# Dummy matmuls in the head, and full inverse matrices for the last four output pairs of a gated long convolution and MLP

## The chip, the cores and the metric

The kernel runs on one core of one Trainium2 chip. The metric is the device time of one execution in microseconds (us). Five engines of that core matter here: PE (TensorE, the matmuls), DVE (VectorE), ACT (ScalarE), POOL (GpSimd) and SP (SyncE, which starts most transfers). PEld is the weight load of PE, which overlaps the matmuls. "Span" is the time from the first to the last instruction of a profiled execution; the time is some 1.8 us longer than the span. "Granted clock" is the TensorE clock that the profile reports, 1.0 being full speed.

## The reference

Two branches on the same input x, of 2048 rows and 640 columns, are mixed by a gate for each row:

```python
def _A_ref(q, k, v, shift_k, ssm_k, ssm_D):      # long convolution
    ...                                          # k_shift: 4-tap causal filter along the rows of k
    kv = k_shift * v
    ...                                          # y: convolution with ssm_k along the 2048 rows, by FFT of 4096
    y = y + kv * ssm_D[None, None, :]
    return q * y

def _B_ref(x, w1, w2, w3, w4):                   # two MLPs, each with a residual
    h = _gelu(_layernorm(x, axis=-1) @ w1)
    ...                                          # hs: four column groups of h shifted by 1, -1, 2, -2 rows, times w2
    x1 = x + hs
    h2 = _gelu(_layernorm(x1, axis=-1) @ w3) @ w4
    return x1 + h2

g = _sigmoid((x * gate_w).sum(-1, keepdims=True))
return g * a + (1 - g) * b                       # a from _A_ref, b from _B_ref, x is A_q
```

## The kernel before

The kernel records some 1,300 operations, each with the engine it runs on, and a list scheduler written in the same file puts the operations of every engine in order. A table of several hundred numbers, called biases, shifts the priority of groups of operations, and a second table, SHIFTS, that of single ones. The order of each engine is then fixed.

The rows are worked on in 16 tiles of 128 rows. In the head, tile after tile is normalised (DVE), transposed (PE) and copied (ACT), and the first layer starts on narrow blocks of columns:

```python
def ln1(t0, t1):
    for t in range(t0, t1):
        ln_bn(t, X[:, t, :])                     # DVE: statistics, two halves of 320
    bn_math(t0, t1)
    for t in range(t0, t1):
        ...
        ts(xn, x, bna[:, t, 0:1], st[0, 5][:, t:t + 1], ALU.subtract, ALU.mult)   # DVE: normalise
        ...                                      # PE: 5 transposes; ACT: one copy out of PSUM
```

In the tail, the convolution comes back from the frequency domain. `G` holds half an inverse transform: four products give a part `pr[:, 0]` that is even about the middle, four more an odd part `pr[:, 1]`. The sum of the parts is one tile of 128 rows, their difference, turned upside down, is the tile that mirrors it. So 8 matmuls give a pair of tiles of 320 columns, with an add, a subtraction and a matmul with a flip matrix. There are 16 such pairs, `k` = 0 to 15:

```python
def final(hh, c, q, k):
    ts_, td = 4 * c + q, 4 * c + 3 - q           # the two tiles of the pair
    ...
    P.dma(sp, qt, rows(A_q))
    act(qt[:, 0], qt[:, 0], ACTF.Copy, scale=gst[3][:, ts_:ts_ + 1])              # ACT: q * g
    pr = ps(2, "inv")[:, :, 0:320]
    for e in range(2):
        mm(pr[:, e], [(G[:, j, e ^ (j // 2), 128 * q:128 * (q + 1)], XF[:, hh, c, j, e ^ (j // 2), :])
                      for j in range(4)])                                         # PE: 4 matmuls
    pf = ps(1, "fl")[:, 0:320]
    for d in (slice(0, 320),) if k < 15 else (slice(0, 160), slice(160, 320)):
        act(ab[:, :, d], pr[:, :, d], ACTF.Copy)                                  # ACT: both parts
        tt(gy[:, 0, d], ab[:, 0, d], ab[:, 1, d], ALU.add)                        # DVE
        tt(ab[:, 0, d], ab[:, 0, d], ab[:, 1, d], ALU.subtract)                   # DVE
        mm(pf[:, d], [(flip, ab[:, 0, d])])                                       # PE
        act(gy[:, 1, d], pf[:, d], ACTF.Copy, scale=gst[3][:, td:td + 1])         # ACT
        for e in (slice(0, 2),) if k < 14 else (slice(0, 1), slice(1, 2)):
            tt(gy[:, e, d], gy[:, e, d], qt[:, e, d], ALU.mult)                   # DVE
            tt(gy[:, e, d], gy[:, e, d], two(X)[:, e, d], ALU.add)                # DVE
            ...                                                                   # out
```

The helpers `tt`, `act` and `mm` record every operation of their kind, so in the profile all matmuls of `mm` have one line, L1230 before and L1234 after; `tt` is L1210 and L1214, `act` L1220 and L1224. `ts` is L1215 and L1219.

## Time and profile before

| | before |
|---|---|
| time, median of 3 runs | 238.98 us (238.97 to 239.32) |
| span of the profiled execution | 237.2 us |
| PE busy, DVE busy, ACT busy | 221.5, 222.1, 177.8 us |
| inverse products and the first flip after them are through on PE | 226.65 us |
| last DVE operation ends | 234.88 us |

The profile's first lines and its stretches are in the prediction below. Three more readings are needed. The first is the shares of the chain of work that ended last:

```profile
PE 44%; DVE 34%; ACT 14%; issue 4%; DMA 2%; SPq 1%; DVEq 0%
```

The chain passes from engine to engine; none has more than half of it. The second is PE's timeline from 199.80 us on (start, length, line and operation, count, and in brackets the idle time before it and the engine that ended it):

```profile
199.80 26.85 PE L1230 MATMUL PSall<-arena 128*128 128x512 bf16 x189
227.02 0.85 PE L1230 MATMUL PSall<-arena 128*128 128x320 bf16 x5 [0.37 <-DVE arena L1210]
232.02 0.58 PE L1230 MATMUL PSall<-arena 128*128 128x320 bf16 x2 [4.15 <-DVE arena L1210]
233.38 0.31 PE L1230 MATMUL PSall<-arena 128*128 128x160 bf16 x1 [0.77 <-ACT arena L1220]
```

PE has no gap until 226.65 us. What comes after are single flip matmuls that wait for a difference from DVE: in this tail DVE works and PE looks on. After the last product there are 9 flips: pairs 8 to 15, one each, and pair 15, which is cut in two, one more. The first of them has just ended at 226.65 us (the stretch from there on still counts it: 9 matmuls, but 8 weight loads); the lines show the other 8. DVE's last stretch, from the same view, ends at 226.49 + 8.39 = 234.88 us:

```profile
226.49 8.39 DVE L1210 TENSOR_TENSOR arena<-arena 128x160 bf16<-128x160 bf16 x31 [0.19 <-ACT arena L1220]
```

The chain in the prediction passes from DVE to "DVEq" at 234.72 us. That is no end of DVE's work: the view books the last operation itself under that name. The third reading is the timeline of PE in the head, from 13 to 21 us:

```profile
14.49 0.73 PE L1445 MATMUL PSall<-arena 128*128 128x128 bf16 x10 [0.30 <-ACT arena L1220]
15.82 4.53 PE L1230 MATMUL PSall<-arena 128*128 128x320 bf16 x37 [0.60 <-DVE arena L1469]
```

L1445 are the transposes. The 37 matmuls from 15.82 us on are the first group of the second layer, and 4.53 us for them is the rate at full clock.

### The profile page before, as it was taken

Reading aid. Unit: us, or ns where it says so; the run is one execution under the profiler, and the core shown is the slowest. Engines: PE = TensorE matmul, PEld = TensorE weight load, DVE = VectorE, ACT = ScalarE, POOL = GpSimd, SP = SyncE. Lnnn points to the kernel's source line nnn. Section 1 sums busy time; section 2 is a strip of 40 time slices with the busy share of each in tenths; the row PEclk is TensorE's granted clock in tenths of the full one; section 3 lists DMA queues with packets and bytes.
Section 4 is the critical chain, followed back from the end, with each engine's and each line's share of the span. In section 5 each row is a group of like instructions: output and inputs, shape, how many; then the busy total and the mean of one; then the engine's idle time right before and its main releaser. Section 6 shows DMA issues by size and latency. Waiting matters only on the chain.

```text
span 237.2 us, 4158 instructions
## 1 busy us (share of the span) xinstructions
PE 221.5 (93%) x1477; PEld 133.4 (56%) x1488; DVE 222.1 (94%) x418; ACT 177.8 (75%) x328; POOL 92.3 (39%) x116
## 2 busy tenths in 40 slices
PE   5789999999999999999999999999999999999931
PEld 2476875556454555544766546764567744677710
DVE  5899999979998999899999799999999799999996
ACT  2288979986889977999999992557897466326972
POOL 0334928932892246230548304643015414152000
PEclk9999999999999999999999999999999999999995
DMA  6999798999989989986264982799989996899825
GB/s 174 348 373 336 147 253 159 116 222 266 212 196 211 260 195 351 298 214 156 67 99 76 187 178 39 130 174 158 267 150 231 158 192 135 172 157 153 219 81 169
DMA packets 64201, 45.54 MB, mean 192 GB/s; under 512 B 28722, under 2 KB 58932, under 8 KB 64180
## 3 DMA queue, kind: packets, MB, share of 16 engines
q1 hardware_dynamic: 57884, 33.36, 56.1%
q0 software_dynamic: 6112, 11.80, 29.8%
q8 instruction: 12, 0.20, 0.3%
q10 hardware_dynamic: 184, 0.11, 0.2%
q14 instruction: 9, 0.07, 0.1%
HBM read 24.29 MB, written 2.62 MB: 113 GB/s over the span
## 4 chain that ended last, share of the span: by engine, by line
PE 44%; DVE 34%; ACT 14%; issue 4%; DMA 2%; SPq 1%; DVEq 0%
PE PSall L1230 43%; DVE arena L1210 27%; ACT arena L1220 14%; DMA arena<-in_A_q_dram 2%; DVE arena L1400 2%; DVE arena L1469 2%; DVE arena L1215 2%; DVE arena L1504 1%; SPq L239 1%; DVE arena L1401 0%; ACT PSall L1220 0%; PE PSall L1445 0%; DVEq L1687 0%; DVEq L453 0%; DVE arena L1354 0%
## 5 line engine op out<-in xcount | busy, mean ns | idle before, releaser
L1230 PE MATMUL PSall<-arena 128*128 128x320 bf16 (+4 forms) x1411 | 212.5, 309 | 8.6 <-DVE arena L1210 5.1
L1210 DVE TENSOR_TENSOR arena<-arena 128x2560 bf16<-128x2560 bf16 (+6 forms) x263 | 185.1, 762 | 6.5 <-ACT arena L1220 4.7
L1230 PEld LDWEIGHTS PSall<-arena 128*128 128x128 bf16 x1422 | 128.5, 98 | 91.5 <-ACT arena L1220 9.1
L1220 ACT ACTIVATE arena<-PSall 128x640 bf16<-128x640 f32 (+5 forms) x187 | 110.9, 651 | 29.3 <-PE PSall L1230 21.3
L1220 ACT ACTIVATE arena<-arena 128x640 bf16<-128x640 bf16 (+3 forms) x74 | 52.0, 733 | 5.5 <-DVE arena L1210 2.9
L239 POOL DMA_DIRECT2D arena<-arena x30 | 31.2, 1102 | 61.1 <-DVE arena L1210 41.9
L1404 POOL TENSOR_TENSOR arena<-arena 128x1 f32<-128x1 f32 (+1 forms) x26 | 24.9, 964 | 35.7 <-DVE arena L1215 35.4
L1215 POOL TENSOR_SCALAR arena<-arena 128x1 f32<-128x1 f32 (+2 forms) x41 | 26.9, 657 | 26.2 <-ACT arena L1220 8.9
L1220 ACT ACTIVATE arena<-PSall,arena 128x640 bf16<-128x640 f32 (+2 forms) x33 | 20.4, 655 | 19.3 <-PE PSall L1230 19.3
L1400 DVE BATCH_NORM_STATS2 arena<-arena 128x6 f32<-128x320 bf16 x32 | 13.8, 477 | 2.7 <-DMA arena<-in_A_q_dram 2.6
L1215 DVE TENSOR_SCALAR arena<-arena 128x1 f32<-128x1 f32 (+2 forms) x45 | 12.4, 299 | 0.6 <-POOL arena L1215 0.2
L1210 POOL TENSOR_TENSOR arena<-arena 128x1 f32<-128x1 f32 (+1 forms) x15 | 10.0, 670 | 3.3 <-DVE arena L1215 2.6
L1256 PE MATMUL PSall<-arena 128*128 128x512 bf16 x24 | 6.7, 448 | 2.4 <-DVE arena L1252 2.4
L1469 DVE TENSOR_SCALAR arena<-arena 32x256 bf16<-32x256 bf16 (+2 forms) x28 | 6.3, 229 | 1.6 <-ACT arena L1220 1.1
L1504 DVE SCALAR_TENSOR_TENSOR arena<-PSall,arena 128x640 bf16<-128x640 f32 x8 | 6.4, 814 | 0.0
L1256 PEld LDWEIGHTS PSall<-arena 128*128 128x128 bf16 x24 | 2.6, 112 | 6.1 <-DVE arena L1252 2.4
L1220 ACT ACTIVATE PSall<-PSall 128x640 f32<-128x640 f32 x8 | 5.7, 711 | 0.0
L1445 PE MATMUL PSall<-arena 128*128 128x128 bf16 x40 | 3.2, 220 | 1.1 <-DVE arena L1215 0.8
L1445 PEld LDWEIGHTS PSall<-arena 128*128 128x128 bf16 x40 | 2.4, 97 | 2.3 <-DVE arena L1215 1.8
L1259 ACT ACT_TABLE_LOAD x1 | 1.3, 1283 | 2.1 <-issue 2.1
L1401 DVE BATCH_NORM_AGGREGATE arena<-arena 128x2 f32<-128x12 f32 x16 | 2.8, 201 | 0.0
L1220 ACT ACTIVATION_READ_ACCUMULATOR arena<-arena 128x1 f32 x8 | 2.1, 257 | 0.0
(23 smaller groups left out, 8.0 us busy)
## 6 DMA issues: line engine op xcount, KB each, us to landing
arena<-arena POOLq DMA_DIRECT2D x14, 640.0 KB, 6.0
arena<-in_A_k_dram SPq DMA_DIRECT2D x14, 400.0 KB, 4.6
arena<-in_A_q_dram SPq DMA_DIRECT2D x20, 160.0 KB, 5.7
arena<-in_A_ssm_k_dram SPq DMA_DIRECT2D x5, 512.0 KB, 4.8
arena<-in_A_v_dram SPq DMA_DIRECT2D x16, 160.0 KB, 2.9
arena<-arena POOLq DMA_DIRECT2D x16, 160.0 KB, 4.2
out_dram<-arena SPq DMA_DIRECT2D x14, 160.0 KB, 2.0
arena<-in_A_q_dram SPq DMA_DIRECT2D x6, 320.0 KB, 6.2
```

Of the source, the lines that this page charges most:

```text
L239: fn = lambda e: e.dma_start(out, in_, **kw)
L1210: P.op(eng, lambda e: e.tensor_tensor(o, real(a), real(b), op), [a, b], [o], dve_ns(o, [a, b], 2) if eng == "dve" else 500)
L1215: P.op(eng, lambda e: e.tensor_scalar(o, real(a), s1, s2, op0=op0, **({} if op1 is None else {"op1": op1})), [a] + aps, [o], dve_ns(o, [a] ...
L1220: P.op("act", lambda e: e.activation(real(o), real(a), f, bias=bias, scale=scale, **({"accum_out": accum} if accum is not None else {})), ...
L1230: fns.append(lambda e, l=l, r=r, i=i: e.matmul(real(o), l, r, start=(i == 0), stop=(i == last)))
L1256: warmed = P.op("pe", [lambda e: e.matmul(real(pw), warm[:, 0:128], warm[:, 128:640], start=True, stop=True)] * 2, [warm], [pw], 856.0 if ...
L1400: P.op("dve", lambda e, o=o, i=i: e.bn_stats(o, i), [i], [o], 400)
L1401: P.op("dve", lambda e: e.bn_aggr(bna[:, t, :], bns[k]), [bns[k]], [bna[:, t, :]], 120)
L1404: P.op("pool", lambda g: g.tensor_tensor(o, a, e, ALU.pow), [a, e], [o], dur)
L1445: P.op("pe", [lambda e, c=c, pb=pb, xn=xn: e.transpose(real(pb)[:, 128 * c:128 * (c + 1)], xn[:, 128 * c:128 * (c + 1)], ident) for c in r ...
L1469: P.op("dve", lambda e, o=hT[q, 4, c0:c0 + n], i=hx[q, :]: e.tensor_scalar(o, i, 1.0, None, op0=ALU.mult), [hx[q, :]], [hT[q, 4, c0:c0 + n ...
L1504: P.op("dve", lambda e: e.scalar_tensor_tensor(x, real(pr), 1.0, x, op0=ALU.mult, op1=ALU.add, accum_out=st[1, 0][:, t:t + 1]), [pr, x], [ ...
```

## The change

It has two intents: to keep PE busy, and its clock up, between the first tiles' first and second layers; and to relieve DVE and ACT in the tail at PE's expense. Besides, the normalisation of tiles 0 to 2 has its priority raised, and both tables of biases have new values throughout, so that the order of every engine is new. The diff, with the number tables left out:

```diff
+        self.boost = 0.0
-        op.bias += self.biases.get(op.grp, 0.0) + self.opb.get(idx, 0.0)
+        op.bias += self.boost + self.biases.get(op.grp, 0.0) + self.opb.get(idx, 0.0)
     ...
+    def keep_warm(n):
+        done = max(o.idx for o in P.ops if o.eng == "pe" and o.grp.startswith("mm1"))
+        pw = ps(1, "warm")
+        for i in range(n):
+            P.op("pe", [lambda e: e.matmul(real(pw), w1[:, 0, 0:128], w1[:, 0, 128:640], start=True, stop=True)] * 2,
+                 [w1], [pw], 432.0).preds.setdefault(done, False)
     ...
+    DIRECT = 12
+    GT = V(oXT, 2048).rearrange("p (e j q m) -> p e j q m", e=2, j=4, q=2)
+    def turn_inverse():
+        for e in range(2):
+            for j in (0, 2):
+                act(GT[:, e, j:j + 2], G[:, j:j + 2, e ^ (j // 2)].rearrange("p j (q m) -> p j q m", q=2)[:, :, :, ::-1],
+                    ACTF.Copy, scale=1.0 - 2.0 * e)
     def final(hh, c, q, k):
     ...
-        act(qt[:, 0], qt[:, 0], ACTF.Copy, scale=gst[3][:, ts_:ts_ + 1])
+        if k < DIRECT:
+            act(qt[:, 0], qt[:, 0], ACTF.Copy, scale=gst[3][:, ts_:ts_ + 1])
     ...
+        if k >= DIRECT:
+            mm(pr[:, 0], halves[0] + halves[1])                                   # 8 matmuls
+            mm(pr[:, 1], [(GT[:, e, j, q], halves[e][j][1]) for e in range(2) for j in range(4)])
+            for e, t in enumerate((ts_, td)):
+                act(gy[:, e], pr[:, e], ACTF.Copy, scale=gst[3][:, t:t + 1])
+        else:
     ...                                          # as before, without the cutting of pair 15
     for sc in range(4):
     ...
+            P.boost = {0: 4e6, 1: 3e6, 2: 1e6}.get(t[0], 0.0)
             at(ln1, *t)
+            P.boost = 0.0
     ...
+                if (sc, k, i) == (0, 0, 1):
+                    at(keep_warm, 4)
```

`keep_warm(4)` makes 8 matmuls of 512 columns whose result nobody reads. `GT` is `G` with its columns reversed, and with the sign of the odd part turned, so that 8 matmuls with it give the mirrored tile at once, without subtraction or flip. `halves` holds the operands of the four even and the four odd products.

## The prediction

> **What bounds the kernel now.** I read the page's busy shares first, then the chain of work that ended last, then busy time by stretches, and last the timeline and the groups of the final 20 us. The first line of the page says that no single engine is the limit:
>
> ```profile
> PE 221.5 (93%) x1477; PEld 133.4 (56%) x1488; DVE 222.1 (94%) x418; ACT 177.8 (75%) x328; POOL 92.3 (39%) x116
> ```
>
> Two engines are near full at once. Stretches show where the remaining idle time lies (columns: PE, PEld, DVE, ACT, POOL busy, clock, DMA share, GB/s):
>
> ```profile
> 0.00:10.00 10.00, 6.75 (x25) 2.62 (x26) 6.15 (x30) 1.49 (x2) 2.12 (x8) 1.00 0.80 254
> 10.00:15.00 5.00, 4.18 (x69) 3.84 (x70) 4.97 (x19) 4.04 (x13) 1.95 (x5) 1.00 1.08 332
> 15.00:20.00 5.00, 4.40 (x41) 3.52 (x38) 4.93 (x18) 4.10 (x9) 1.33 (x5) 1.00 1.05 378
> ...
> 180.00:210.00 30.00, 29.89 (x189) 18.47 (x189) 28.65 (x36) 16.29 (x29) 9.56 (x10) 1.00 0.90 167
> 210.00:220.00 10.00, 10.00 (x76) 7.11 (x75) 9.60 (x12) 5.21 (x10) 4.73 (x5) 1.00 0.95 165
> 220.00:226.65 6.65, 6.65 (x49) 4.57 (x47) 6.17 (x20) 6.65 (x15) 0.00 (x0) 1.00 0.75 199
> 226.65:235.00 8.35, 1.75 (x9) 0.64 (x8) 8.23 (x31) 4.44 (x11) 0.00 (x0) 0.73 0.40 119
> ```
>
> From 10 us to 226.65 us, taken as one stretch, PE is busy 213.00 of 216.65 us and DVE 207.71. So the middle has 3.65 us of PE gaps and 8.9 us of DVE gaps to give, no more. What is left is the head (PE does only warm-up matmuls before 9.98 us) and the tail: after 226.65 us PE is nearly empty while DVE is full. The chain names the tail's owner, in order of time (start, length, engine and line):
>
> ```profile
> 213.74 2.97 DVE arena L1210 x3
> 216.71 0.02 issue
> 216.73 9.73 ACT arena L1220 x20
> 226.47 0.02 issue
> 226.49 8.24 DVE arena L1210 x30
> 234.72 0.15 DVEq L1687
> ```
>
> The last chained product ends near 218.2 us; from 218.50 to 234.72 DVE does nothing but the output pairs, and ACT is full from 220 us to 226.65. The groups of instructions between 218 and 237 us give the prices:
>
> ```profile
> L1210 DVE TENSOR_TENSOR arena<-arena 128x640 bf16<-128x640 bf16 x18 | 7.9, 492 | 0.3 <-ACT arena L1220 0.3
> L1210 DVE TENSOR_TENSOR arena<-arena 128x320 bf16<-128x320 bf16 x20 | 6.0, 324 | 0.4 <-ACT arena L1220 0.3
> L1220 ACT ACTIVATE arena<-PSall 128x640 bf16<-128x640 f32 x8 | 5.5, 682 | 0.0
> L1220 ACT ACTIVATE arena<-PSall,arena 128x320 bf16<-128x320 f32 x9 | 4.2, 534 | 2.6 <-PE PSall L1230 2.6
> L1210 DVE TENSOR_TENSOR arena<-arena 128x160 bf16<-128x160 bf16 x12 | 2.2, 244 | 0.2 <-ACT arena L1220 0.2
> ```
>
> Busy over count gives what one costs in a full row: 0.44 us for 640 elements, 0.30 for 320, 0.18 for 160. The timeline gives the matmul's price: 123 matmuls of 128x320 took 16.87 us from 209.78 us on, 0.137 us each.
>
> **What the skill says.** "Perfetto Trace Analysis", section Identifying the Most-Contended Engine, warns that matmul busy share does not tell the distance to the roofline. Checked: the page's and the groups' matmul counts come to about 488,000 columns, which at the 2.4 GHz of "TensorE: Matmul & The Clock Gate" is an estimated 203 us, 86% of the span. PE really has little to give in the middle. The same TensorE page (section What's actually happening) says that the array runs at half rate until it has been busy for about 3.4 us, and drops back after an idle window of that length. The trace agrees at the start: the first 7 warm-up matmuls of 512 columns take 3.06 us, 0.44 us each. But after 9.98 us the longest PE gap is 0.83 us, and in 15.82 to 20.2 us 36 matmuls of 320 and 256 columns take 4.42 us, near full rate. So there was no cold stretch in the head for dummy matmuls to cure. "ScalarE: Activation LUTs", section What ACT_TABLE_LOAD costs, prices an activation with immediates at 186 ns + 0.833 ns per element, less 93 ns of overlap, and 93 ns for a pointer operand. That is 546 ns for 320 elements with a pointer; the trace has 534.
>
> **The change, part by part.**
>
> Head. Raised priority for the first tiles' statistics, and 8 dummy matmuls of 512 columns. Before, DVE took the statistics of tiles 2 and 3 (7.10 to 9.1 us) ahead of normalising tile 0 at 9.12 us. In the changed order tile 0's normalisation stands behind one statistics half of tile 2, so it can start near 7.10 + 0.48 = 7.6 us, 1.5 us earlier. The dummies cost at most 8 x 0.215 = 1.7 us (estimate from the page's 215.7 ns), and stand after the second narrow first-layer block and among the next blocks, where before PE had gaps of 0.30 and 0.60 us. I count them as nothing to +0.3 us. What is the 1.5 us worth? PE has 3.65 us of gaps left after 9.98 us, 1.4 us of them before 16 us, so an earlier start can be passed on only while DVE keeps up, and DVE is busy 29.3 of 30 us from 10 to 40 us. I put the head at -0.6 us, and this is a guess between 0 and -1.5.
>
> Tail, the last four output pairs (12 to 15). The sum and difference of the two half products, and the flip, go into the matrix product by using all 8 products with ready-made matrices for each output half.
> - DVE: pairs 12 to 14 lose an add and a subtract of 320: 6 x 0.30 = 1.8 us. Pair 15 had 12 operations of 160 (2.2 us) and keeps 4 of 320 (1.2 us): 1.0 us. In all -14 operations and -2.8 us, all on the path.
> - PE: 16 products in place of 8 and a flip: 28 more in four pairs, 28 x 0.137 = +3.8 us, none hidden, as PE has no gap from 209.78 to 226.65 us.
> - ACT: pairs 12 to 14 lose 0.55 (scaling q) + 0.68 + 0.53 and pay 2 x 0.53, so 0.69 each; pair 15 saves 1.1: -3.2 us in the tail. Making the turned matrices adds 4 copies of 512 elements, an estimated 0.52 us each by the ACT page, 2.1 us in all; the new order has them by the third block of the second MLP, within 180 to 210 us, where ACT is busy 16.3 of 30 us. Off the path.
>
> Two ends compete. DVE: 234.72 - 2.8 = 231.9 us. PE: 226.65 + 3.8 = 230.5, then the last scaled eviction 0.53, multiply and add 0.60, hand-overs about 0.2: 231.8 us. They meet, so the tail gives nearly the whole 2.8 us and PE becomes a joint bound. Output after DVE's end stays 237.2 - 234.7 = 2.5 us, and time over span 239.0 - 237.2 = 1.8 us. 231.9 + 2.5 + 1.8 = 236.2, less 0.6 for the head: **235.6 us**.
>
> Middle. All scheduling biases were replaced, so every engine's order is new. The work is the same; the gaps may move by a microsecond either way. I expect zero, with that spread.
>
> **The rivals.**
> 1. PE takes over the tail. The order has 90 matmuls (12.3 us) behind the last chained product, in place of 48 of inverse and 9 of flip, and three flips stand ahead of the last two pairs, waiting for DVE. If DVE is late with those, PE stalls and then still owes 24 matmuls, 3.3 us. For it: PE already lagged by some 13 matmuls at 218.2 us. Against it: DVE has 14.4 us of work there and its differences for those flips come in the first 8 us. It would make 237 to 238 us.
> 2. The head passes on in full, because PE is the real bound, and the new order closes some of the 3.65 us. For it: PE's 98% in the middle. Against it: DVE's saturation until 40 us and waits on ACT around 98 to 111 us in the chain. It would make 233.5 to 234.5 us.
> 3. The dummies or the new middle order cost more than the tail gains: about 239 us. The dummies alone are too short for that.
>
> **Range and chances.** Centre 235.6; the head is uncertain by 0.9, the middle by 1.3, the tail by 1: together about 1.9 us. Range 233.3 to 237.8. Over 2% faster means under 234.2 us, which needs rival 2 or a lucky middle: 0.21. Over 2% slower would need 243.8: 0.02. Within 2%: 0.77.
>
> **What would show it.** Right: DVE has 14 operations less; PE works on to about 230 us at full clock and the gap after 227 us is gone; DVE's last operation ends near 231.3 us; tile 0 is normalised near 7.6 us; the dummies fill gaps. Wrong: the last pairs' DVE operations wait for PE by over 1 us (rival 1); PE's busy time from its first real matmul to its last falls short of its stretch by much less or much more than 3.65 us (the middle moved); matmuls between 10 and 25 us run at half rate (then the dummies matter after all).

## The result, and the profile after

| | before | changed |
|---|---|---|
| time, median of 4 runs | 238.97 us (238.3 to 239.32) | 236.59 us (the three fast ones 236.01 to 236.88, median 236.3) |
| span, PE busy, DVE busy | 237.2, 221.5, 222.1 us | 235.0, 226.9, 219.4 us |
| DVE instructions | 418 | 404 |
| PE's last matmul ends | flips until 233.69 us | 230.54 us |
| last DVE operation ends | 234.88 us | 232.68 us |

The ratio is 0.9896, with a 95% interval of 0.986 to 0.9931: 1% faster. Ratios, here and below, are the mean time of one kernel's fast runs over that of the other's in the same rounds, so they are not quite the ratio of the medians that are quoted.

One of the four executions, the profiled one, took 299.73 us at a granted clock of 0.755 throughout. It explains nothing here. The same kernel was therefore run again ("after_again", the first experiment), and its fast profile is the one that is read from here on. First the busy shares, from the top of its page:

```profile
PE 226.9 (97%) x1523; PEld 138.0 (59%) x1523; DVE 219.4 (93%) x404; ACT 176.7 (75%) x326; POOL 83.2 (35%) x116
```

Before, PE and DVE were level; now PE leads DVE by 7.5 us. PE's records went from 1477 to 1523, but before some matmul records were missing (1488 weight loads beside 1477 matmuls). By weight loads it is 35 more: 8 dummies and 27 in the tail, where pair 15 had two half flips. Busy time by stretches (columns as in the prediction: PE, PEld, DVE, ACT, POOL busy, clock, DMA share, GB/s):

```profile
0.00:10.00 10.00, 7.57 (x31) 3.28 (x32) 5.92 (x28) 2.53 (x4) 1.62 (x7) 1.00 0.79 248
10.00:15.00 5.00, 4.86 (x64) 3.66 (x61) 4.90 (x19) 3.43 (x12) 1.76 (x4) 1.00 1.09 341
15.00:20.00 5.00, 4.92 (x42) 3.94 (x43) 4.94 (x19) 3.45 (x8) 1.36 (x4) 1.00 1.06 374
...
210.00:220.00 10.00, 10.00 (x76) 7.22 (x74) 9.85 (x17) 6.38 (x14) 2.97 (x4) 1.00 0.91 170
220.00:226.65 6.65, 6.65 (x51) 4.71 (x50) 5.62 (x18) 4.73 (x10) 0.00 (x0) 1.00 0.57 173
226.65:235.00 8.35, 3.89 (x29) 2.57 (x27) 6.01 (x18) 3.66 (x8) 0.00 (x0) 0.88 0.52 157
```

In the head PE's gaps between 10 and 20 us are down from 1.42 to 0.22 us. In the tail it is the last two rows that changed: ACT, which was full from 220 to 226.65 us, is busy 4.73 of 6.65 us, DVE has 18 operations after 226.65 us where it had 31, and PE has 29 where it had 9. PE's timeline from 199.82 us on is a single line:

```profile
199.82 30.73 PE L1234 MATMUL PSall<-arena 128*128 128x320 bf16 x225
```

The gaps of 4.15 and 0.77 us for the flips are gone, and PE works through to 230.54 us. The whole stretch from the first real work on, taken as one:

```profile
10.00:230.50 220.50, 219.25 (x1494) 134.74 (x1491) 211.25 (x369) 173.28 (x321) 81.55 (x110) 1.00 0.88 192
```

PE is idle for 1.25 us of 220.50 us; before it was 3.65 us up to 226.65. The shares of the chain say the same, and then the chain itself from 205 us on (start, length, engine and line):

```profile
PE 75%; DVE 13%; ACT 5%; POOL 2%; DMA 2%; issue 2%; SPq 1%; DVEq 0%
```

```profile
204.87 20.80 PE PSall L1234 x153
225.67 0.02 issue
225.69 0.95 ACT arena L1224 x2
226.65 0.02 issue
226.67 4.67 DVE arena L1214 x13
231.34 0.08 issue
231.42 1.03 DVE arena L1214 x4
232.45 0.24 DVEq L1716
```

Read from below: the end is still set by 18 DVE operations in a row, from 226.67 us on (17 under DVE, the last one booked as DVEq). But what those wait for is no longer DVE's and ACT's own work since 214 us, as before; it is PE, whose products are chained without a break until 225.67 us. PE's last matmul ends at 230.54 us, DVE's last operation 2.1 us later, and neither has much idle time left (from 10 to 230.5 us PE 1.25 us, DVE 9.25 us). DVE's timeline shows two waits for ACT ahead of that end:

```profile
221.77 4.65 DVE L1214 TENSOR_TENSOR arena<-arena 128x640 bf16<-128x640 bf16 x14 [0.73 <-ACT arena L1224]
226.67 6.01 DVE L1214 TENSOR_TENSOR arena<-arena 128x640 bf16<-128x640 bf16 x18 [0.25 <-ACT arena L1224]
```

What ACT did then it had itself begun late: before these evictions it stood idle for 0.52 and 1.23 us, waiting for PE.

### The profile page after: what moved, and what is told of

Read it like the earlier page. It is cut to its first block, busy times and chain, and to the rows that moved or that the text cites. A ratio compares the mean times of both kernels' runs of the same rounds, so it can differ in the third digit from the quotient of the medians.

```text
span 297.9 us, 4232 instructions
## 1 busy us (share of the span) xinstructions
PE 291.3 (98%) x1523; PEld 159.2 (53%) x1523; DVE 221.7 (74%) x404; ACT 183.1 (61%) x326; POOL 78.9 (26%) x116
## 4 chain that ended last, share of the span: by engine, by line
PE 98%; DVE 1%; ACT 0%; issue 0%; ACTq 0%; DVEq 0%
PE PSall L1234 93%; PE PSall L1260 3%; PE PSall L1449 1%; PE PSall L1458 1%; DVE arena L1256 0%; DVE arena L1214 0%; ACT arena L1224 0%; ACTq L1716 0%; DVEq L1716 0%; DVE arena L1245 0%; DVE arena L1244 0%; DVE arena L1246 0%; DVE arena L1247 0%; DVE arena L1250 0%; DVE arena L1251 0%
## 5 line engine op out<-in xcount | busy, mean ns | idle before, releaser
L1234 PE MATMUL PSall<-arena 128*128 128x320 bf16 (+4 forms) x1449 | 279.1, 367 | 0.0
L1234 PEld LDWEIGHTS PSall<-arena 128*128 128x128 bf16 x1449 | 152.8, 111 | 125.8 <-issue 65.1
L1214 DVE TENSOR_TENSOR arena<-arena 128x2560 bf16<-128x2560 bf16 (+4 forms) x249 | 184.1, 789 | 46.0 <-ACT arena L1224 41.1
L1224 ACT ACTIVATE arena<-PSall 128x512 bf16<-128x512 f32 (+5 forms) x182 | 109.6, 635 | 65.9 <-PE PSall L1234 57.2
L1224 ACT ACTIVATE arena<-arena 128x640 bf16<-128x640 bf16 (+4 forms) x74 | 49.1, 699 | 0.1
L1224 ACT ACTIVATE arena<-PSall,arena 128x320 bf16<-128x320 f32 (+1 forms) x36 | 22.1, 644 | 43.5 <-PE PSall L1234 43.4
L1219 POOL TENSOR_SCALAR arena<-arena 128x1 f32<-128x1 f32 (+2 forms) x41 | 19.3, 476 | 66.1 <-DVE arena L1515 41.5
L1408 POOL TENSOR_TENSOR arena<-arena 128x1 f32<-128x1 f32 (+1 forms) x26 | 20.7, 809 | 32.9 <-DVE arena L1219 32.4
L1260 PE MATMUL PSall<-arena 128*128 128x512 bf16 x24 | 8.3, 512 | 2.4 <-DVE arena L1256 2.4
L1214 POOL TENSOR_TENSOR arena<-arena 128x1 f32<-128x1 f32 (+1 forms) x15 | 8.2, 551 | 2.2 <-DVE arena L1219 1.7
L1260 PEld LDWEIGHTS PSall<-arena 128*128 128x128 bf16 x24 | 2.9, 126 | 6.2 <-issue 3.6
L1449 PE MATMUL PSall<-arena 128*128 128x128 bf16 x40 | 3.8, 242 | 0.0
L1449 PEld LDWEIGHTS PSall<-arena 128*128 128x128 bf16 x40 | 2.9, 104 | 1.5 <-issue 1.0
L1458 PE MATMUL PSall<-arena 128*128 128x512 bf16 x8 | 2.8, 468 | 0.0
```

The source lines that it names most:

```text
L1214: P.op(eng, lambda e: e.tensor_tensor(o, real(a), real(b), op), [a, b], [o], dve_ns(o, [a, b], 2) if eng == "dve" else 500)
L1219: P.op(eng, lambda e: e.tensor_scalar(o, real(a), s1, s2, op0=op0, **({} if op1 is None else {"op1": op1})), [a] + aps, [o], dve_ns(o, [a] ...
L1224: P.op("act", lambda e: e.activation(real(o), real(a), f, bias=bias, scale=scale, **({"accum_out": accum} if accum is not None else {})), ...
L1234: fns.append(lambda e, l=l, r=r, i=i: e.matmul(real(o), l, r, start=(i == 0), stop=(i == last)))
L1260: warmed = P.op("pe", [lambda e: e.matmul(real(pw), warm[:, 0:128], warm[:, 128:640], start=True, stop=True)] * 2, [warm], [pw], 856.0 if ...
L1408: P.op("pool", lambda g: g.tensor_tensor(o, a, e, ALU.pow), [a, e], [o], dur)
```

## The experiments

All kernels below gave the right result. Each call to the chip also ran the kernel before in the same rounds; its medians there were 239.08, 239.32, 239.1 and 238.94 us, and every ratio is against those of its own call. The calls ran on three different chips, so runs of different calls are best compared by their ratios.

Two theories were to be told apart at first. The prediction's theory is that the tail gives nearly all of the 2.8 us and the head a little. The rival theory is that PE had become the bound by then, so that the tail gives less than DVE loses, and what head and middle free on PE counts.

### after_again: the changed kernel once more

There is no edit.

> The changed kernel, unaltered, for a profile at full clock (the one on record fell on an execution with a granted clock of 0.755). All theories: 236.3 us in its fast runs. Tail theory: DVE never waits for PE by more than 0.3 us after 219 us, and DVE's last operation ends near 231.5 us. PE theory (PE took over the tail): the last pairs' DVE operations wait for PE by over 1 us in all, and PE's last matmul ends within 1.5 us of DVE's end.

Measured: 236.89 us (236.61 to 237.53), ratio 0.9911 (0.9882 to 0.994), clock 0.996. This is the size of the whole effect: 0.9 to 1%. Neither theory's signs came as named. DVE's waits of 0.73 and 0.25 us, at one remove for PE, are more than the tail theory allowed and just short of the PE theory's 1 us; PE ends 2.1 us before DVE, not within 1.5 us; and DVE's end, 232.68 us, is over 1 us later than the tail theory's 231.5.

### no_dummies: the order kept, the dummy matmuls taken out

```diff
     sched = P.schedule({...})
+    gone = {o.idx for o in P.ops if o.grp.startswith("keep_warm")}
+    sched = [o for o in sched if o.idx not in gone]
+    for o in sched:
+        o.preds = {p: v for p, v in o.preds.items() if p not in gone}
```

> The changed kernel without the 8 dummy matmuls; every engine's order is otherwise frozen as it was. Tail theory (dummies only fill gaps): same as the changed kernel within 0.3 us. Rival (dummies keep the clock up): half-rate matmuls between 10 and 25 us and at least 0.7 us slower than the changed kernel. Third possibility, that they delay real work: faster by 0.4 us or more.

Measured: 236.61 us (236.25 to 237.63), ratio 0.9905 (0.9872 to 0.9938), clocks 0.995 to 1.0 in all six executions. The profile has a gap of 1.09 us in place of the dummies, and another of 0.34 us, and no matmul became slower. So in the changed kernel's own order the dummies cure nothing that was seen in these six executions. They cost 0.28 us by the medians, which the intervals do not separate from nothing.

### before_tail and after_old_tail: one part exchanged, the priorities as they were

```diff
 # before_tail: the kernel before, with the new last four pairs and its own biases
+    at(turn_inverse)
-    def final(hh, c, q, k):      # old
+    def final(hh, c, q, k):      # new, DIRECT = 12
 # after_old_tail: the changed kernel, with the old last four pairs and the new biases
-    at(turn_inverse)
-    def final(hh, c, q, k):      # new
+    def final(hh, c, q, k):      # old
```

> The kernel before with the new last four pairs alone: old priorities, so old order up to the tail (order agrees until 314 of 396 operations on DVE and 296 of 354 on PE). Tail theory: 2.8 us under before, 236.2 us. PE theory: PE becomes the bound and 1.0 to 1.7 us are left, 237.3 to 238.0 us. Order theory (the gain comes from the new order of head and middle): within 0.4 us of before, 238.7 us.

> The changed kernel with the old code for the last four pairs: new head, dummies and new middle order, old tail. Tail theory: 0.6 us under before, 238.4 us. PE theory: 1.0 to 1.5 us under before, since then the rest must give what the tail does not. Order theory: 236.5 us, as the changed kernel.

Measured: before_tail 246.77 us (246.39 to 247.33), ratio 1.0324 (1.0287 to 1.0361); after_old_tail 243.28 us (241.6 to 243.64), ratio 1.016 (1.0123 to 1.0196). The priorities are not quite as they were: 57 and 37 of nearly 1,200 single shifts, almost all of them on the last operations, fall away because these are numbered anew. Both runs missed by far what either theory said. PE's timeline of before_tail from 221 us on shows why:

```profile
221.18 0.45 PE L1230 MATMUL PSall<-arena 128*128 128x320 bf16 x2 [1.57 <-DVE arena L1210]
222.86 3.97 PE L1230 MATMUL PSall<-arena 128*128 128x320 bf16 x16 [1.24 <-ACT arena L1220]
228.34 9.41 PE L1230 MATMUL PSall<-arena 128*128 128x320 bf16 x68 [1.50 <-ACT arena L1220]
```

PE stands still three times, 4.31 us in all, for a DVE and an ACT that are at something else, and has 68 matmuls left at 228.34 us. After the second stop, from 222.8 us on, the granted clock is also down to 0.50 for some 3.4 us. The work is the new tail's, but its order is that of biases that were found for the old tail. In after_old_tail PE waited the other way round, 5.83 us at 236 us for the last difference from DVE. This two-by-two comparison compares orders and not operations. A part can only be judged with an order of its own.

### tail_tuned and rest_tuned: one part, with the last stages' order searched anew

The same two exchanges, but the order up to the last stages is kept exactly, and the priorities of the last stages' operations were searched at random with the kernel's own scheduler.

```diff
 # both
+    TAIL = {886: 200863, 887: 173069, ...}       # priorities of single operations of the last stages
+    for i, v in TAIL.items():
+        P.opb[i] = P.opb.get(i, 0.0) + v
 # tail_tuned: kernel before with the new last four pairs
 # rest_tuned: changed kernel (head, dummies, middle) with the old last four pairs
```

> The kernel before with the new last four pairs, and the priorities of the last stages (from the third block of the second MLP on) searched anew; PE's order ahead of them is exactly that of before. It stands in for before_tail, whose loss could be its untuned order. Prediction's sum: 2.8 us under before, 236.2 us. Revised theory (PE has 36 matmuls left to do after 226.65 us in place of the 28 that I counted, since the flips of before also came after it: 226.65 + 4.9 = 231.6, then 1.9 us to DVE's end as in the changed kernel, 233.5 against 234.7): 1.2 us under before, 237.8 us. Order theory (the new code of the last pairs is worth nothing): 239 us or more.

> The changed kernel with the old last four pairs, and the priorities of the last stages searched anew: new head, dummies and middle with a fitted old tail. Prediction: 0.6 us under before, 238.4 us. Revised theory (the new head and middle bring PE 1 us forward, but the old tail ends on DVE and ACT and cannot use it): 0 to 0.5 us under before, 238.6 to 239.1 us. Order theory: 236.9 us.

Measured: tail_tuned 238.33 us (237.89 to 238.68), ratio 0.9951 (0.9924 to 0.9977); rest_tuned 238.98 us (238.06 to 239.55), ratio 0.9981 (0.9953 to 1.0008). PE's timeline of tail_tuned from 176 us on, and then that of rest_tuned:

```profile
175.64 55.99 PE L1282 MATMUL PSall<-arena 128*128 128x512 bf16 x379
```

```profile
175.80 50.67 PE L1287 MATMUL PSall<-arena 128*128 128x320 bf16 x334
230.87 0.58 PE L1287 MATMUL PSall<-arena 128*128 128x320 bf16 x2 [4.39 <-DVE arena L1267]
232.85 0.32 PE L1287 MATMUL PSall<-arena 128*128 128x160 bf16 x1 [1.40 <-DVE arena L1267]
```

In tail_tuned PE works without a gap to 175.64 + 55.99 = 231.63 us, 1.1 us later than in the changed kernel's profile, and DVE's last operation ends at 234.06 us, only 0.8 us earlier than before. So the new tail by itself is worth 0.5%, some 1.0 to 1.2 us, not 2.8 us: PE limits it. In rest_tuned PE is through its products, and 6 of the 9 flips, at 226.47 us and then waits for DVE's differences, as in the kernel before; DVE's last operation ends at 234.17 us, 0.7 us earlier. The rest of the change by itself, with the best old tail that this search found, is worth 0.2%, which its interval does not tell from nothing. The two parts' gains sum to 0.7%, the whole is 0.9 to 1%; the intervals are too wide to say that there is more in the whole than in the parts.

Against before_tail the order alone took the same operations from 246.77 to 238.33 us: 8.4 us, several times what the whole change gains.

### dummies_doubled: what PE time costs in the head

```diff
     sched = P.schedule({...})
+    for o in sched:
+        if o.grp.startswith("keep_warm"):
+            o.fns = o.fns * 2
```

> The changed kernel with 16 dummy matmuls in place of 8, every engine's order frozen. If dummies only fill gaps that PE has anyway: within 0.4 us of the changed kernel. If PE is the bound from the head to the tail, so that what does not fit a gap is paid in full: 8 x 0.215 = 1.7 us less the gap of 0.22 us left there, 1.2 to 1.7 us slower, about 238.3 us.

Measured: 239.2 us (238.59 to 239.39), ratio 0.9988 (0.9964 to 1.0012). That is 2.3 us above the changed kernel by the medians and 1.8 us by the two ratios, for 8 more dummies, which the prediction estimated at 1.7 us. PE's last matmul ends at 232.83 us, 2.3 us later than in the changed kernel's profile, so the delay goes through the whole execution undiminished. PE's idle time from 40 to 180 us is 2.24 us of 140, where the changed kernel has 0.85 us; but rest_tuned, whose order is the same there, has 1.57 us, so this does not show that the delay grew on the way. PE time in the head is paid for in full at the end. That alone does not prove that PE is the bound of the whole kernel: in tile0_early, below, whose tail still ends on DVE, 1.68 us that PE loses in the head arrive in full as well.

### head_only and tile0_early: the earlier tile 0 in the kernel before

Both freeze the kernel before in its own order on every engine and reorder the head alone. head_only puts the groups of the head in the changed kernel's order:

```diff
+    P.seq = {'pe': [...], 'act': [...], 'dve': [...], ...}   # order before, head groups refilled in the changed order
```

> The kernel before, its order frozen except that the first tiles' statistics, normalisation and first-layer work stand in the changed kernel's order (no dummies, no other change). Prediction: 0.6 us under before, 238.4 us, tile 0 normalised about 1.5 us earlier. Rival (the 1.5 us pass on in full): 237.5 us. Revised theory (the old tail ends on DVE, whose work is not less): within 0.4 us of before.

Measured: 243.87 us (243.47 to 244.42, 5 runs), ratio 1.0185 (1.0157 to 1.0212). This is a faulty experiment: the mixed order makes PE wait 2.27 us for a copy on DVE, so it says nothing on the head's worth. But it shows something else. Two stretches of its busy time:

```profile
20.00:25.00 5.00, 2.29 (x17) 0.98 (x16) 4.90 (x20) 3.67 (x9) 2.33 (x6) 0.92 0.96 292
25.00:30.00 5.00, 5.00 (x43) 3.04 (x42) 3.30 (x7) 1.26 (x3) 1.01 (x2) 0.50 0.01 5
```

After a stretch in which PE was busy 2.29 of 5 us, the granted clock is 0.50 for the next 5 us. So in this run the clock was halved after a gap in the head. The profile of the kernel before shows that only in its tail, after the gap of 4.15 us. But of its 44 executions in these four calls one, of 240.93 us, has a mean clock of 0.977 where the others have 0.983 to 0.991, as the slow executions of tile0_early have; it was not profiled. tile0_early changes less:

```diff
 # order of DVE, 7 to 10 us
-  statistics of tile 2 (2 halves), of tile 3 (2 halves), aggregates, normalise tile 0, normalise tile 1
+  statistics of tile 2 (1 half), normalise tile 0, statistics of tile 2 (1 half), normalise tile 1, statistics of tile 3
 # order of PE: the transposes of tiles 0 and 1 move forward among the warm-up matmuls
```

> The kernel before, order frozen, with only two things moved: tiles 0 and 1 are normalised on DVE ahead of the statistics of tiles 2 and 3, and PE transposes them among its warm-up matmuls. It replaces head_only, in which my frozen order made PE wait 2.3 us for a copy. Prediction's step: tile 0 normalised 1.5 us earlier, 0.6 us under before. Rival (the head passes on in full): 1.5 us under. Revised theory (DVE is saturated until 40 us and PE's next inputs come from it in the same order): same as before within 0.3 us.

Measured: 239.85 us (238.38 to 241.18), ratio 1.0028 (0.9982 to 1.0074). Tile 0 is normalised at 7.71 us in place of 9.12, the same step forward as in the changed kernel (7.86 us), and nothing is gained. PE's timeline from 13 us on:

```profile
14.71 0.73 PE L1451 MATMUL PSall<-arena 128*128 128x128 bf16 x10 [1.23 <-DVE arena L1221]
16.02 6.21 PE L1236 MATMUL PSall<-arena 128*128 128x320 bf16 x37 [0.58 <-DVE arena L1475]
```

PE is done with the first blocks sooner, waits 1.23 us for the normalisation of the next tiles (L1221) and 0.58 us more, and starts the second layer at 16.02 us, 0.2 us later than before: DVE is full and sets the pace. Then the same 37 matmuls take 6.21 us in place of 4.53, at a granted clock of 0.66 over 15 to 20 us. That is the profiled execution, of 240.9 us. Three of the six executions have a mean clock of 0.977 to 0.983 and take 240.69 to 241.18 us; the other three have 0.987 to 0.99 and take 238.38 to 239.0 us. So with the earlier tile 0 there is a gap after which the clock falls in some executions, and without that it is worth next to nothing here.

### after_plus and after_ref: a version that might beat both

after_plus is no_dummies with the last stages searched anew, after_ref the changed kernel on the same chip.

```diff
 # after_plus
+    TAIL = {...}                                  # as above
+    sched = [o for o in sched if o.idx not in gone]   # as in no_dummies
```

> The changed kernel without dummies, and with the priorities of its last stages searched anew: a candidate to beat both. If PE's columns are the bound, 0 to 0.5 us under the changed kernel, 236.3 to 236.6 us.

> The changed kernel, unaltered, on the same chip as the candidate: 236.8 us.

Measured: after_plus 236.58 us (236.3 to 236.82), ratio 0.9899 (0.987 to 0.9928); after_ref 236.97 us (236.37 to 237.54), ratio 0.9913 (0.9882 to 0.9944). after_plus is 0.4 us faster than the changed kernel in the same rounds, which these six executions of each do not tell from nothing, and no faster than no_dummies (236.61 us). The clock of after_plus stayed at 0.996 to 1.0 without any dummies.

### tile0_dummies: dummies where tile0_early has its gaps

```diff
 # tile0_early, and
+                if (sc, k, i) == (0, 0, 1):
+                    at(keep_warm, 3)              # 4 matmuls ahead of the transposes of tiles 2 and 3, 2 ahead of the second layer
```

> tile0_early with 6 dummy matmuls of 512 columns put into its two PE gaps: 4 ahead of the transposes of tiles 2 and 3 (gap 1.23 us), 2 ahead of the first second-layer group (gap 0.58 us). Half of tile0_early's executions ran near 240.9 us with a granted clock of 0.977 to 0.983, and its profile shows a clock of 0.66 from 15 to 20 us. If dummies keep the clock up: no execution above 239.6 us, and the clock is 1.00 in each stretch from 10 to 40 us; median 238.9 us. If the dropped clock has another cause: again about half of the executions near 240.9 us. If the earlier tile 0 is worth the 0.6 us predicted once the clock holds: 238.4 us.

Measured: 238.39 us (237.64 to 238.99), ratio 0.9972 (0.995 to 0.9994), clocks 0.985 to 0.991. PE's timeline from 13 us on:

```profile
13.90 1.03 PE L1460 MATMUL PSall<-arena 128*128 128x512 bf16 x4
14.76 0.72 PE L1451 MATMUL PSall<-arena 128*128 128x128 bf16 x10
15.32 0.59 PE L1460 MATMUL PSall<-arena 128*128 128x512 bf16 x2
16.07 4.54 PE L1236 MATMUL PSall<-arena 128*128 128x320 bf16 x37 [0.15 <-DVE arena L1482]
```

L1460 are the dummies. They fill the gaps, and the 37 matmuls of the profiled execution take 4.54 us again. In all six executions the mean clock shows no sign of a fall in the head (the kernel before has 0.984 to 0.991 too, because of its tail: its stretches have 1.00 up to 226.65 us and 0.73 after it). By the two ratios it is 0.6% faster than tile0_early, and its 238.39 us is what was named in advance if the earlier tile 0 is worth 0.6 us once the clock holds. This fits what the dummies can be for, an insurance for an order with gaps; with three falls in six executions against none in six, on another chip, it is not settled. In the order of the changed kernel no fall was seen in 12 executions without dummies (no_dummies and after_plus).

## Why the prediction was right or wrong

- **DVE's share of the tail** was right in its size: 14 operations less, and 2.7 us less busy time against 2.8. The end of DVE moved by 2.2 us, from 234.88 to 232.68, as two short waits for ACT (0.73 and 0.25 us) came in.
- **PE's share of the tail is the term that was mis-sized.** The working took 226.65 us as PE's end before and added 28 matmuls, "226.65 + 3.8 = 230.5". But it counted in those 28 that the flips of the last pairs go away, and those flips lay after 226.65 us anyway, as did three of the four flips of pairs 8 to 11, which stay and have to be done earlier now. What must be added is 32 products and these 3 flips: 35 x 0.137 = 4.8 us, so 231.4 us. tail_tuned measured 231.63. (The 36 in its expectation count the flip that has just ended at 226.65 us.) So "the tail gives nearly the whole 2.8 us" was wrong: by itself it gives 1.0 to 1.2 us.
- **That PE's end was nevertheless at 230.54 us,** as predicted to within a tenth, is luck: two errors cancel (and after_ref's profile of the same kernel has 230.82 us). Head and middle brought PE forward by 231.63 - 230.54 = 1.1 us in these profiles, and the sign that the prediction named for a moved middle came: 3.65 us of idle time became 1.25, of which the 8 dummies took 1.7 us by the prediction's estimate and real work the rest; and the first layer starts at 10.76 us in place of 11.23.
- **"They meet"** held, and for longer than meant: PE is in the chain without a break from 205 to 225.67 us, DVE from 226.67 us to the end. From PE's last matmul to DVE's last operation it took 2.1 us, where the working had 1.33. Part of it shows in ACT: the last two evictions both ran after PE's end, 0.95 us for the two, where one was counted with 0.53.
- **The head's -0.6 us** was called a guess. Its first step was right: tile 0 is normalised one statistics half after its wait for the data ends, at 7.45 + 0.41 = 7.86 us (predicted 7.6, from 7.10). What that is worth is not settled: nothing in tile0_early, and with dummies 0.3%, which is the guess's size, in one run. Head, dummies and middle together were worth 0.2% with the old tail, and brought PE 1.1 us forward with the new one. How the latter divides between head and middle stays open. The idle time points to the middle, which the prediction put at zero: from 10 to 40 us PE's fell by 1.37 us, less than the dummies' 1.7, and from 40 to 210 us, where there are none, by 1.04 us. But in after_ref's profile the latter is 0.65 us.
- **The dummies at 0 to +0.3 us:** no_dummies says 0.28 us, not told from zero. "There was no cold stretch in the head for dummy matmuls to cure" was right of the profiled execution of the kernel before, and short-sighted as an argument: in the runs with an earlier tile 0, another part of the same change, there are gaps after which the clock can fall. The 0.83 us gap that it names ends at 9.98 us; after that none ahead of the tail is over 0.60 us.
- **ACT's turned matrices** were busy for 2.4 us against the estimated 2.1, off the path. "ScalarE: Activation LUTs", section What ACT_TABLE_LOAD costs, fits: its formula gives 613 ns for one such copy and 520 ns less the overlap; the trace has a mean of 614 ns, and the two copies that stand in a row start 0.52 us apart (180.08 and 180.60 us). The prediction's 546 ns for 320 elements leaves the overlap out that its sentence names; with it the formula gives 453 ns, and evictions in a row start 0.41 us apart in the trace of the kernel before (227.26, 227.68 us). ACT's total went down by 1.1 us; the working's -3.2 + 2.1 makes the same -1.1.
- **The end:** 2.3 us from DVE's last operation to the end of the span, before and after, and 1.87 us from there to the time (predicted 1.8). The predicted 2.5 us were counted from the chain's mark at 234.72.
- **The sum:** -3.4 us predicted, -2.4 us on record. The missing microsecond is this: the uncounted matmuls, 231.4 in place of 230.5 us, put PE's end 0.9 us later; the way from there to DVE's end was 0.8 us longer; head and middle gave 0.3 to 0.5 us more than the guess.
- **The rivals:** the first, that PE takes over the tail, was half right; PE took over everything up to 225.67 us, and DVE's two waits at the end, 0.98 us in all, go back to PE by way of ACT. The second, the head in full, did not come: no time under 236.0 us was seen. The third did not come either; it needed dummies twice as many (239.2 us).

What stays open: at what gap the clock falls, what head and middle gave each, and why one execution ran at a clock of 0.755.

## What to carry to other kernels

When work is moved from one full engine to another, work out the new end of the receiving engine from all that will have to lie before its end, including small work that until now waited in the other engine's shadow: here 7 matmuls miscounted in that way cost about 1 us of the 2.8 us that were expected of the tail. Judge a part of a change only with an order tuned for it: the same operations in an order tuned for others were 8.4 us slower, more than three times what the change gains. Dummy matmuls can pay only where a gap of PE lets the clock fall; where they fill no gap, they are paid for at the end: here 8 more cost 1.8 to 2.3 us.

## What the Trainium skill lacked or had wrong

- Page "TensorE: Matmul & The Clock Gate", section HAM oscillation, gives as the abstract rule that there should be no PE gaps longer than about 3.4 us. Here the clock also fell after shorter ones: to 0.66 on average over 15 to 20 us after gaps of 1.23 and 0.58 us (in three of six executions by their mean clocks), and to 0.50 over 25 to 30 us in a stretch whose longest gap was 2.27 us; in before_tail to 0.50 from 222.8 us on, after gaps of 1.57 and 1.24 us. A gap of 1.09 us with one of 0.34 us never did in six executions. The length of the slow spell does agree with its section What's actually happening: the 37 matmuls lost 6.21 - 4.53 = 1.68 us, which at half rate is a spell of some 3.4 us. What the page lacks is a figure for how much idle time within a window is enough.
- Same page, section Seeing it yourself: it says that one or two busy cores never trip the limiter that takes the clock to 13/16. One execution of this program on one core had a granted clock of 0.755 over its whole span of 297.9 us. That is not 13/16 (0.81) either. What else ran on the chip is not known, so this is an observation without a cause.
- No page says that the end of an engine's busy stretch has to be read together with its small instructions that wait behind another engine after it. Here those were 8 flip matmuls after 226.65 us, of which 3 had to be done earlier in the changed kernel and were not counted.
